# Agent attention with a SoLU layer on one core: u copied by transfer and transposed in rounded fp32, three of five tile pairs transposed on TensorE, and the buffers and queues around that

## The chip, the cores and the metric

The kernel runs on one core of a Trainium2 chip. The metric is the device time of one execution in microseconds, given as the median of the runs. PE is the matrix engine (TensorE), DVE the vector engine, ACT the scalar engine, POOL the general engine (GpSimd), and SP the engine that issues the transfers (DMAs).

## The reference

Four batches of 12,608 tokens with 128 channels; 49 agents per batch; a feed-forward width of 1,024.

```python
a2k = sm(agents, k); agent_v = a2k @ v        # per batch: 49 x 128
x = sm(q, agents) @ agent_v                   # sm: softmax of the scaled product
h = x @ w_in
solu = h * softmax(h)
ln = (solu - mean) / sqrt(var + 1e-06) * g_ln
out = ln @ w_out
```

`w_in` and `w_out` come as 64-bit floats and are converted to 32-bit ones on the chip.

## The kernel before, in words

All work is cut into operations that the class `Plan` (L26) puts in order when the program is built: each `op(engine, function, cost, due, dependencies)` has a price and a due time, and a list scheduler writes the instructions of each engine in the order that comes out. On the chip every engine runs its own list strictly in that order. SP's list of transfers is ordered in the same way, and a transfer whose source isn't ready holds all transfers behind it on SP. Four PSUM banks `px` are handed out by the plan; two further tiles `ph` (two banks each) hold the rows of `h`.

**Phase A** (`phase_a`, once per batch) walks over k and v in 12 chunks of 1,024 tokens and a rest: load k and v (`kop`, `vop`), logits (L465), running maximum (L470), exp (L491), transpose (L498), copy to SBUF (L504), product with v (L514), and the sum with a factor (L523). At the end the product of the agents' values with `w_in` is written as a high and a low part, `mh` and `ml` (L585, L590), each 128 x 1024 in rounded fp32 (fp32r). `mh` and `ml` have two buffers. For the first batch (the head), nothing else runs meanwhile but the conversion of the weights.

**Phase B** (`phase_b`, once per 8 token tiles) makes the softmax p of the queries over the agents: logits (L694), normalised values in `pack` (L722, POOL), two transposes per four tiles (L729), a copy from PSUM (L737, ACT), a split into high and low part on POOL (L743, L748), and four to eight transfers on SP that put them, one below the other, into `pT` (L767).

**Phase C** runs over 396 tiles of 128 tokens:
- `c_h` (L824): four matmuls give 128 x 1024 of h in `ph`; `c_max` (L828, DVE), `c_exp` (L838, ACT, into a tile `e`), `c_u` (L843, DVE): u = h * e / 1024 in a tile `u` (two buffers); `c_sq` (L849, ACT): the sum of squares.
- Tiles go in pairs, and pairs have two kinds; `PAT` gives the order. A **Z** pair transposes u on TensorE (`c_t`, L856, eight 128 x 128 blocks of fp32 per tile), ACT copies the result to SBUF (`c_ev`, L907), POOL splits it into a high and a low part in fp32r (`c_sph` L916, `c_spl` L920), and 24 matmuls of 256 columns per pair (`c_w`, L937) multiply with the split `w_out`. A **Y** pair is transposed in 32 x 32 blocks by DVE (`c_tb`, L863), the blocks are put in their places by 16 transfers per group of four tiles (`c_mv`, L871), and 32 fp32 matmuls per group (`c_wy`, L877) multiply with `w_out`.
- Groups of four tiles (two pairs of a kind, called units) share a chain of small POOL operations that gives the factor 1/std per token (`c_rstd`, L951 to L972). A Z group turns it with DVE (L976), sends it to DRAM and reads it back as a row repeated on all partitions (`send` L980, `sent` L984); `c_fin` (L1020, DVE) multiplies and `c_out` (L1025) stores. A Y group needs it per partition: POOL makes `dy` (L1002), TensorE sums (L1007), ACT or DVE copies it (`yp`, L1011), and `c_fy` (L885 on ACT, L887 on DVE) multiplies.

With the order ZYZY, and Z for the last four pairs, there are 102 Z pairs and 96 Y pairs.

Of the kernel before, what the change touches and what calls it, by code (L numbers as in the profile page):

```python
# [19 lines left out]
class Op:  # L20


    __slots__ = ("eng", "fn", "cost", "due", "left", "outs", "deps", "take", "free", "bank", "start", "end", "by", "ready", "kind", "shy")


class Plan:  # L26
# [11 lines left out]

    def __init__(self, banks):
# [4 lines left out]
        self.kind = 0  # L44

# [14 lines left out]
    def push(self, o):  # L60
        o.ready = {}
        for e in o.eng:
            o.ready[e] = max([0.0] + [d.end + (self.LAT.get(d.by + e, 0.2) if d.by != "S" else 0.0) for d in o.deps])
            self.cand[e].append(o)

    def run(self, idle=None):
        while True:
            best = None
            for e, ops in self.cand.items():
                if not ops:  # L70
                    continue
                free = [b[0] for b in self.banks if b[0] is not None]
                first = min(free) if free else None
                at, opts, low = self.at[e], [], None
                for o in ops:
                    s = max(at, o.ready[e])
                    if o.take:
                        if first is None:
                            continue
                        s = max(s, first)  # L80
                    opts.append((s, o))
                    low = s if low is None else min(low, s)
                if low is None:
                    continue
                near = [z for z in opts if z[0] <= low + self.EPS[e]]
                if e == "P" and self.kind == 2:
                    near = [z for z in opts if z[0] <= low + self.HOLD and z[1].kind == 2] or near
                s, o = min(near, key=lambda z: z[1].due)
                if o.shy > 0.0:
                    s, o = min((z for z in opts if z[0] <= s + o.shy), key=lambda z: z[1].due)  # L90
                if best is None or s < best[0]:
                    best = (s, e, o)
            if best is None:
                break
            s, e, o = best
            for z in o.eng:
                self.cand[z].remove(o)
            if o.take:
# [5 lines left out]
            o.start, o.by = s, e  # L104
            if e == "S":
                hold, size, lag = o.cost
                self.at[e] = s + hold
# [24 lines left out]
PAT = "ZYZY"  # L132
# [18 lines left out]
def kernel(  # L151
# [15 lines left out]
    P = 128  # L167
# [9 lines left out]
    CPR = 5.63  # L177
    UTB = 3
# [9 lines left out]
    BD0 = 5.03  # L188
    BD1 = 15.85
    BD2 = 1.88  # L190
    BD3 = -20.87
    BD4 = -3.24
    BD5 = 3.07
    DH = -9.08
    DMX = 6.59
    DEX = 1.64
    DU_ = -21.8
    DSQ = 15.3
    DT = -0.97
    DEV = 13.79  # L200
    DLD = 12.64
    DSP = 16.84
    DW = 13.2
    DR = 15.79
    DF_ = 37.93
    OUTD = 20.02
    OUTC = -69.6
    VA = 3
    VA1 = 12
    QA = 22.03  # L210
    WA = -7.03
    VLAG = 0.74
    PTB = 4
    SHY = 0.31
    DHR = 5.82
    DHL = -9.02
    DMXR = 19.87
    DMXL = 0.06
    DEXR = -2.43
    DEXL = -3.57  # L220
    DUR = -30.17
    DUL = 17.14
    DSQR = -54.86
    DSQL = 4.96
    DTR = -20.36
    DTL = -14.12
    DEVR = -17.55
    DEVL = 7.51
    DLDR = -20.48
    DLDL = -18.62  # L230
    DSPR = -1.34
    DSPL = -11.65
    DWR = -2.28
    DWL = 3.97
    RBL = 2.38
    ASP = 0.86
    MZ = 5.66
    B7G = True
    B7 = 7.35
    DTB = 4.24  # L240
    DMV = -0.75
    DMS = 0.0
    MVC = 2
    DWY = 11.65
    DWS = 4.05
    YC = 2
    DFY = 5.09
    DTBR = -5.14
    DTBL = -8.26
    ASTART = -4.09  # L250
    AEND = 0.95
# [20 lines left out]
    make_identity(nc, ident)  # L272
    ones = const.tile([P, P], F32, name="ones")
# [13 lines left out]
    def pair_f64(dst, names):  # L287
# [5 lines left out]
        def tmp():  # L293
            for k, tg in (("s", "e"), ("a", "e"), ("e", "u"), ("m", "u")):
                t = epool.tile([P, 2, HW], I32, tag=tg, bufs=2, name=f"c{k}_{names}")
# [39 lines left out]
    def load_out():  # L335
        nc.sync.dma_start(out=g_sb, in_=g_ln)
        for h in range(2):
            wd = words["out", h] = mpool.tile([P, HW, 2], I32, tag="mh" if h == 0 else "ml", name=f"wd_out{h}")
# [6 lines left out]
    def conv_out():  # L345
# [8 lines left out]
        def sums(q):  # L354

            n = NF >> (q + 1)
            if q == 0:
                pm["s"] = epool.tile([P, NF // 2, C], F32, tag="sq", bufs=1, name="ws")
# [32 lines left out]
    for i in range(2):  # L391
        pk = const.tile([P, GT, AP2], F32, name=f"pack{i}")
        nc.gpsimd.memset(pk, 0.0)
# [10 lines left out]
    fold32 = const.tile([P, SQB], F32, name="fold32")  # L404
    nc.vector.tensor_reduce(out=fold32, in_=ident.rearrange("p (a c) -> p c a", c=SQB), op=ALU.add, axis=AX.X)
# [838 lines left out]
```

## Time and profile before

| | |
|---|---|
| median of 3 runs | 1501.4 us (1495.41 to 1503.94) |
| the profiled execution | 1496.0 us, span 1494.2 us, granted clock 0.995 |
| PE busy | 1447.1 us, 97% of the span |
| DVE busy | 1371.5 us, 92% |
| ACT busy | 1291.3 us, 86% |
| POOL busy | 1110.3 us, 74% |
| q1 (the transfers of the kernel) | 63.1% of the 16 DMA engines' time |

The profile shows one execution. A busy time is the union of the engine's instructions, so overlapping parts of neighbours count once; a matmul's own duration holds the way through the array, so that neighbours overlap. The pace of matmuls is read from the chain that ended last, where a piece is the time from one group of instructions to the next.

### The profile page before, as it was taken

What the parts mean: (1) busy time and instruction counts of PE and PEld (TensorE: products, weight loads), DVE (VectorE), ACT (ScalarE), POOL (GpSimd) and SP (SyncE); (2) the same over time, 40 slices, a digit from 0 to 9 for tenths busy, and PEclk for the clock granted to TensorE, in tenths of its full rate; (3) what the DMA queues carried; (4) which work ended last, traced back from release to release, by engine and by line L of the source; (5) the groups of instructions that cost most, each with busy time, mean ns of one, the idle gap of its engine ahead of it and who ended that gap; (6) DMA issues with size and microseconds to landing.
All of it is one profiled execution on the core that took longest, in us unless ns stands there. A gap on an engine that the chain in (4) does not pass through costs nothing.

```text
span 1494.2 us, 34108 instructions
## 1 busy us (share of the span) xinstructions
PE 1447.1 (97%) x11954; PEld 1285.0 (86%) x11954; DVE 1371.5 (92%) x1987; ACT 1291.3 (86%) x2536; POOL 1110.3 (74%) x1569
## 2 busy tenths in 40 slices
PE   8889999999999999999999999899999999999999
PEld 5668889898988989989887888789889898989998
DVE  7799999999999999999998898699999999999996
ACT  4688989889988988899887898688899999999995
POOL 2667787788778777787786677677788888888875
PEclk9999999999999999999999999999999999999999
DMA  9565676676577668756657655567546656566461
GB/s 371 163 179 156 177 186 160 174 184 153 144 194 202 165 179 215 181 137 158 155 140 200 184 156 157 147 175 206 138 118 157 152 126 166 137 154 162 114 155 57
DMA packets 142698, 247.72 MB, mean 166 GB/s; under 512 B 26048, under 2 KB 80320, under 8 KB 142528
## 3 DMA queue, kind: packets, MB, share of 16 engines
q1 hardware_dynamic: 142528, 245.54, 63.1%
q8 instruction: 96, 1.57, 0.5%
q14 instruction: 74, 0.61, 0.1%
HBM read 92.77 MB, written 26.05 MB: 80 GB/s over the span
## 4 chain that ended last, share of the span: by engine, by line
PE 56%; ACT 13%; DVE 10%; DMA 10%; issue 5%; SPq 4%; POOL 2%; DVEq 0%; ACTq 0%; POOLq 0%
PE ph L824 15%; PE px L877 14%; PE px L937 11%; PE px L856 6%; ACT e L838 5%; DVE u L843 4%; DMA rB<-dr 4%; ACT sq L849 4%; DVE nm L828 3%; PE px L465 3%; SPq L871 3%; PE px L514 3%; DMA dr<-yr 2%; ACT uT L907 2%; PE px L694 2%
## 5 line engine op out<-in xcount | busy, mean ns | idle before, releaser
L849 ACT ACTIVATE sq<-u,su 128x1024 bf16<-128x1024 f32 x396 | 460.7, 1163 | 53.4 <-DVE u L843 49.2
L843 DVE SCALAR_TENSOR_TENSOR u<-ph,e 128x1024 f32<-128x1024 f32 x396 | 474.6, 1217 | 29.4 <-ACT e L838 13.6
L838 ACT ACTIVATE e<-ph,nm 128x1024 f32<-128x1024 f32 x396 | 442.8, 1124 | 60.6 <-DVE nm L828 58.9
L828 DVE TENSOR_REDUCE nm<-ph 128x1 f32<-128x1024 f32 x396 | 467.8, 1206 | 28.2 <-PE ph L824 26.8
L920 POOL TENSOR_TENSOR uL<-uT,uH 128x1024 fp32r<-128x1024 f32 (+1 forms) x198 | 470.7, 2377 | 14.5
L877 PE MATMUL px<-w,uY 128*128 128x128 f32 x3072 | 383.0, 276 | 1.7 <-ACT uT L907 1.0
L877 PEld LDWEIGHTS px<-w,uY 128*128 128x128 f32 x3072 | 365.9, 192 | 8.7 <-ACT uT L907 2.3
L824 PE MATMUL ph<-mh,pT 128*128 128x512 f32 x792 | 336.5, 425 | 8.6 <-DVE u L843 5.4
L824 PE MATMUL ph<-ml,pT 128*128 128x512 f32 x792 | 312.8, 395 | 0.0
L916 POOL TENSOR_SCALAR uH<-uT 128x1024 fp32r<-128x1024 f32 (+1 forms) x198 | 207.6, 1048 | 99.2 <-ACT uT L907 99.0
L937 PE MATMUL px<-uH,wH 128*128 128x256 f32 x816 | 238.7, 292 | 0.6 <-POOL x L957 0.3
L863 DVE STREAM_TRANSPOSE tb<-u 128x1024 f32<-128x1024 f32 x192 | 237.2, 1238 | 1.3
L937 PE MATMUL px<-uL,wH 128*128 128x256 f32 x816 | 235.7, 289 | 0.0
L907 ACT COPY uT<-px 128x512 f32<-128x512 f32 x394 | 220.8, 595 | 16.7 <-PE px L856 12.9
L937 PE MATMUL px<-uH,wL 128*128 128x256 f32 x816 | 235.0, 288 | 0.0
L856 PE MATMUL px<-ident,u 128*128 128x128 f32 x1632 | 223.0, 274 | 6.8 <-DVE ob L1020 4.0
L856 PEld LDWEIGHTS px<-ident,u 128*128 128x128 f32 x1632 | 191.2, 141 | 33.4 <-DVE ob L1020 5.1
L824 PEld LDWEIGHTS ph<-mh,pT 128*128 128x128 f32 x792 | 149.8, 189 | 43.7 <-DVE u L843 13.5
L824 PEld LDWEIGHTS ph<-ml,pT 128*128 128x128 f32 x792 | 150.1, 189 | 19.5 <-DVE ml L590 0.3
L937 PEld LDWEIGHTS px<-uH,wL 128*128 128x128 f32 x816 | 153.8, 189 | 5.0 <-issue 2.3
L937 PEld LDWEIGHTS px<-uH,wH 128*128 128x128 f32 x816 | 153.9, 189 | 4.8 <-issue 1.3
L937 PEld LDWEIGHTS px<-uL,wH 128*128 128x128 f32 x816 | 154.1, 189 | 4.2 <-issue 1.1
(132 smaller groups left out, 1595.9 us busy)
## 6 DMA issues: line engine op xcount, KB each, us to landing
uY<-tb SPq DMA_DIRECT2D x768, 128.0 KB, 2.9
pT<-pn SPq DMA_DIRECT2D x392, 64.0 KB, 2.2
qt<-in_qT_dram SPq DMA_DIRECT2D x48, 512.0 KB, 4.4
kt<-in_kT_dram SPq DMA_DIRECT2D x36, 512.0 KB, 4.4
vt<-in_v_dram SPq DMA_DIRECT2D x36, 512.0 KB, 4.8
rB<-dr SPq DMA_DIRECT2D x50, 256.0 KB, 3.7
out_dram<-ob SPq DMA_DIRECT2D x50, 256.0 KB, 2.6
out_dram<-oy SPq DMA_DIRECT2D x48, 256.0 KB, 2.8
```

Source lines behind the costliest of these rows:

```text
L824: nc.tensor.matmul(ph[:, sl], lhs, bmats[b]["mh" if m == 0 else "ml"][:, sl], start=(m == 0), stop=(m == 1))
L828: nc.vector.tensor_reduce(out=nms[x], in_=phs[x], op=ALU.max, axis=AX.X, negate=True)
L838: nc.scalar.activation(out=es[x], in_=phs[x], func=AF.Exp, bias=nms.pop(x), accum_out=st[G]["S"][:, j : j + 1])
L843: nc.vector.scalar_tensor_tensor(out=u, in0=phs[x], scalar=INV, in1=es[x], op0=ALU.mult, op1=ALU.mult, accum_out=su)
L849: nc.scalar.activation(out=sq, in_=u, func=AF.Square, bias=su, scale=-float(DF), accum_out=st[G]["Q"][:, j : j + 1])
L856: nc.tensor.transpose(pt[:, kf * P : (kf + 1) * P], us[x][0][:, k0 * P : (k0 + 1) * P], ident)
L863: nc.vector.transpose(to, us[x][0].rearrange("p (k r c) -> p k r c", r=GT, c=SQB))
L877: nc.tensor.matmul(st[G]["po"][:, a * P : (a + 1) * P], yb[G][1][:, a, kf].rearrange("p x c -> p (x c)"), w2[:, kf, :], start=(kf == 0), s ...
L907: nc.scalar.copy(out=rr[x][:, hf * 4 : hf * 4 + 4, :], in_=pt)
L916: nc.gpsimd.tensor_scalar(out=uH, in0=rr[x][:, k0:k1, :], scalar1=1.0, scalar2=0.0, op0=ALU.mult, op1=ALU.add)
L920: nc.gpsimd.tensor_tensor(out=uL, in0=rr[x][:, k0:k1, :], in1=uH.bitcast(F32), op=ALU.subtract)
L937: nc.tensor.matmul(po, wt[:, kf, :], ut[:, kf, :], start=(q == 0), stop=(q == WM - 1))
```

## The change

- The order of pairs becomes ZYZYZ. With Z for the last four pairs there are 120 Z pairs and 78 Y pairs.
- A Z tile's u is copied by a transfer (`c_cp`, 512 KB) from the tile `u` to a tile `uR` of type fp32r (three buffers), and TensorE transposes `uR` against an fp32r identity. `u` has three buffers, `uT` four. The squares of `c_sq` are written over the tile `e` instead of a tile of their own.
- p is split into its high and low part before it is turned: `b4`, `b4h`, `b4l` on POOL; one transpose per tile in fp32r instead of one per two tiles; ACT's copy of 512 columns writes `pT`. The split after the transpose and the transfers of `pT` are gone.
- The factor of a Y group goes through DRAM too (`send`, and `senty`, which reads it as 4-byte elements); `dy`, its matmul and its copy are gone. `rB` has three buffers, and `c_fin` writes its result over `rB`.
- In the head all loads of k are listed ahead of those of v, with other buffers, and the transposed values of all chunks are kept.
- `mh` and `ml` have one buffer: their writing waits for the last `c_h` of the batch before.
- The plan gets operations of the kind "SA", a transfer that SP or ACT may issue; ACT is offered it 30 us after it is ready, and only behind an operation of over 1 us. The due times of most operations get other values.

```diff
-PAT = "ZYZY"
+PAT = "ZYZYZ"
...
+            if e == "A" and o.eng == "SA":
+                o.ready[e] += self.SLACK
...
-    UTB = 3
+    UTB = 4
+    RB_ = 3
+    UBF = 3
...
-    MVC = 2
+    MVC = 1
...
-    mpool = ctx.enter_context(tc.tile_pool(name="mpool", bufs=2))
+    mpool = ctx.enter_context(tc.tile_pool(name="mpool", bufs=1))
...
+    rpool = ctx.enter_context(tc.tile_pool(name="rpool", bufs=RB_))
...
+    identR = const.tile([P, P], F32R, name="identR")
+    nc.vector.tensor_copy(out=identR, in_=ident)
...
-                old = M1.get(c - 1) if not head else M1.get(c - 5 - c % 4)
+                old = M1.get(c - 1) if not head else None
...
-            old = M2.get(c - 1) if not head else M2.get(c - 5 - c % 4)
+            old = M2.get(c - 1) if not head else M1[3] if 4 <= c < 8 else M1[7] if 8 <= c < NCK else None
...
+        for c in range(NC if head else 0):
+            kop(c)
...
-            o9 = op("A", st(f4h, hf), 0.571, at(z + 0.8 + 0.4 * hf), [o8, l0, last_h.get(b - 2)] + mdone[b])
+            o9 = op("A", st(f4h, hf), 0.571, at(z + 0.8 + 0.4 * hf), [o8, l0, last_h.get(b - 1)] + mdone[b])
...
+        def b4h(q):
+            m, d, _ = cut(q)
+            nc.gpsimd.tensor_scalar(out=packs[q][:, :m, 0, :A], in0=d, scalar1=1.0, scalar2=0.0, op0=ALU.mult, op1=ALU.add)
+
+        def b4l(q):
+            m, d, _ = cut(q)
+            nc.gpsimd.tensor_tensor(out=packs[q][:, :m, 1, :A], in0=d, in1=packs[q][:, :m, 0, :A].bitcast(F32), op=ALU.subtract)
+
         def b5(q, px):
...
-            for j in range(0, m, 2):
-                nc.tensor.transpose(px[:, j * AP2 : (j + 2) * AP2], packs[q][:, j : j + 2, :].rearrange("p j a -> p (j a)"),
-                                    ident)
+            for j in range(m):
+                nc.tensor.transpose(px[:, j * P : (j + 1) * P].bitcast(F32R), packs[q][:, j].rearrange("p i a -> p (i a)"), identR)
 
         def b6(q):
...
+            pt = pTs[b, t0 // GT + q] = bpool.tile([P, GT * P], F32R, tag="pT", bufs=PTB, name=f"pT{b}_{t0}_{q}")
+            nc.scalar.copy(out=pt[:, : m * P], in_=r.pop(("pt", q))[:, : m * P])
...
-        sq = epool.tile([P, DF], BF16, tag="sq", bufs=1, name=f"sq{x}")
+        sq = es.pop(x).bitcast(BF16)[:, :DF]
...
+    def c_cp(x, e):
+        rr[x, "u"] = rpool.tile([P, DF], F32R, tag="uR", name=f"uR{x}")
+        port[e].dma_start(out=rr[x, "u"].bitcast(F32), in_=us[x][0])
...
-            nc.tensor.transpose(pt[:, kf * P : (kf + 1) * P], us[x][0][:, k0 * P : (k0 + 1) * P], ident)
+            nc.tensor.transpose(pt[:, kf * P : (kf + 1) * P].bitcast(F32R), rr[x, "u"][:, k0 * P : (k0 + 1) * P], identR)
...
+        def senty(e):
             yp = st[G]["yp"] = tiny.tile([P, GT], F32, tag="yp", name=f"yp{G}")
...
+            port[e].dma_start(out=yp, in_=r["dr"].rearrange("j p -> (j p)").rearrange("(a p) -> p a", p=P))
...
-        U[x] = op("D", F(c_u, x), 1.21, at(x, DU_, DUR, DUL), [EX[x], T.get((x - 2, 0)), T.get((x - 2, 1)), TBT.get(x - 2), SQ.get(x - 2)])
+        U[x] = op("D", F(c_u, x), 1.21, at(x, DU_, DUR, DUL), [EX[x], CP.get(x - UBF), TBT.get(x - UBF), SQ.get(x - UBF)])
...
+            CP[x] = op("SA", F(c_cp, x), (0.5, 0.524, 0), at(x, DCP, DTR, DTL), (cout if zx < RB_ else []) + [U[x], T.get((xo, 0)), T.get((xo, 1))])
             for hf in range(2):
-                T[x, hf] = op("P", F(c_t, x, hf), 0.435, at(x, DT, DTR, DTL) + 0.02 * hf, [U[x]] + buf, take=True)
+                T[x, hf] = op("P", F(c_t, x, hf), 0.28, at(x, DT, DTR, DTL) + 0.02 * hf, [CP[x]] + buf, take=True)
```

## Rows read from the trace of the kernel before

**Rows 1.** The page's first part: busy time of each engine, its share of the span, and its instructions.
```profile
span 1494.2 us, 34108 instructions
PE 1447.1 (97%) x11954; PEld 1285.0 (86%) x11954; DVE 1371.5 (92%) x1987; ACT 1291.3 (86%) x2536; POOL 1110.3 (74%) x1569
```

**Rows 2.** Busy time by stretch: from and to, length, then the busy us of PE, PEld, DVE, ACT and POOL with their instructions, the granted clock, the DMA share and GB/s. The first row is the kernel between head and tail, the second its busiest long stretch.
```profile
100.00:1440.00 1340.00, 1310.92 (x10813) 1181.20 (x10812) 1252.59 (x1779) 1191.21 (x2332) 1033.14 (x1455) 1.00 0.64 163
...
1000.00:1300.00 300.00, 296.85 (x2454) 270.04 (x2453) 287.90 (x404) 273.23 (x530) 243.35 (x337) 1.00 0.61 151
```

**Rows 3.** The chain that ended last, from 640 to 673 us: start, length, engine, tile, line and number of instructions. Length by number is the pace. (An fp32 matmul of L877 is two records.)
```profile
640.37 0.12 PE px L1007 x2
...
664.44 1.79 PE px L877 x16
666.23 1.85 PE ph L824 x8
...
669.00 2.39 PE px L937 x20
671.39 0.87 PE px L856 x8
672.26 0.22 PE px L729 x2
```

**Rows 4.** Waits and what followed one. First who waited for whom: us in total, number of times, longest us; then two stretches in the form of Rows 2.
```profile
DVE ob L1020 <- DMA rB<-dr: 30.2, 18, 8.3
...
PE px L498 <- DVE ob L1020: 8.6, 2, 7.6
...
920.00:940.00 20.00, 12.41 (x94) 11.41 (x93) 11.41 (x18) 11.74 (x24) 8.69 (x15) 0.93 0.39 119
940.00:960.00 20.00, 20.00 (x161) 17.31 (x160) 17.18 (x26) 16.29 (x33) 13.95 (x17) 0.89 0.72 173
```

**Rows 5.** Groups of instructions on DVE by line and shape: count, busy us and mean ns of one, then idle time before them.
```profile
L863 DVE STREAM_TRANSPOSE tb<-u 128x1024 f32<-128x1024 f32 x192 | 237.2, 1238 | 1.3
...
L1020 DVE TENSOR_TENSOR ob<-px,rB 128x512 f32<-128x512 f32 x50 | 34.2, 684 | 30.2 <-DMA rB<-dr 30.2
...
L976 DVE STREAM_TRANSPOSE yr<-ycol 128x32 f32<-128x32 f32 x50 | 9.9, 197 | 0.0
...
L887 DVE TENSOR_TENSOR oy<-px,yp 128x512 f32<-128x512 f32 x14 | 9.5, 682 | 2.0 <-PE px L877 2.0
```

**Rows 6.** The same view, ACT. (The four instructions of L885 serve one group.)
```profile
L907 ACT COPY uT<-px 128x512 f32<-128x512 f32 x394 | 220.8, 595 | 16.7 <-PE px L856 12.9 <-POOL z L963 1.7 <-POOL pack L722 0.6
...
L885 ACT ACTIVATE oy<-px,yp 128x128 f32<-128x128 f32 x136 | 38.7, 370 | 0.4
L737 ACT COPY pf<-px 128x256 f32<-128x256 f32 x100 | 38.1, 387 | 7.3 <-PE px L729 7.2
...
L1011 ACT COPY yp<-px 128x4 f32<-128x4 f32 x34 | 5.6, 165 | 0.7 <-PE px L1007 0.6
```

**Rows 7.** The same view, POOL.
```profile
L920 POOL TENSOR_TENSOR uL<-uT,uH 128x1024 fp32r<-128x1024 f32 x196 | 468.1, 2389 | 14.3
...
L916 POOL TENSOR_SCALAR uH<-uT 128x1024 fp32r<-128x1024 f32 x196 | 206.3, 1053 | 99.2 <-ACT uT L907 99.0
...
L748 POOL TENSOR_TENSOR pn<-pf,pn 128x256 fp32r<-128x256 f32 x100 | 73.7, 737 | 7.7
...
L743 POOL TENSOR_SCALAR pn<-pf 128x256 fp32r<-128x256 f32 x100 | 41.0, 410 | 31.0 <-ACT pf L737 29.0 <-DMA out_dram<-ob 1.5
```

**Rows 8.** Transfers. First the queue's packets, MB and share of the 16 engines; then SP's own timeline (start, length, line, transfer, count): one burst of 16; then two stretches in the form of Rows 2, the first with a load to and stores from 128 partitions, the second in that burst; last, issues by line with KB of one and the median us to landing.
```profile
q1 hardware_dynamic: 142528, 245.54, 63.1%
...
724.01 10.74 SPq L871 DMA_DIRECT2D uY<-tb  x16
...
722.00:724.00 2.00, 2.00 (x13) 1.63 (x12) 2.00 (x5) 1.61 (x4) 1.92 (x2) 1.00 0.99 362
730.00:732.00 2.00, 2.00 (x13) 1.25 (x12) 2.00 (x3) 2.00 (x4) 1.92 (x2) 1.00 0.97 217
...
uY<-tb SPq DMA_DIRECT2D x768, 128.0 KB, 2.9
pT<-pn SPq DMA_DIRECT2D x392, 64.0 KB, 2.2
...
kt<-in_kT_dram SPq DMA_DIRECT2D x36, 512.0 KB, 4.4
```

**Rows 9.** The head and the end of a phase A: a piece of the chain that ended last (six matmuls of the first tiles' `c_h`), SP's last loads of v in the head, and the groups that write `mh` and `ml`.
```profile
58.07 1.57 PE ph L824 x6
...
35.14 3.14 SPq L459 DMA_DIRECT2D vh<-in_v_dram  x3
...
L590 DVE SCALAR_TENSOR_TENSOR ml<-px,rs,mh 128x512 fp32r<-128x512 f32 x8 | 5.9, 739 | 1.4 <-ACT mh L585 1.4
L585 ACT ACTIVATE mh<-px,rs 128x512 fp32r<-128x512 f32 x8 | 5.5, 694 | 0.7 <-DVE wL L377 0.7
```

More of the change, by code (lines that the diff above doesn't have):

```diff
@@ L20 @@
 class Op:
-    __slots__ = ("eng", "fn", "cost", "due", "left", "outs", "deps", "take", "free", "bank", "start", "end", "by", "ready", "kind", "shy")
+    __slots__ = ("eng", "fn", "cost", "due", "left", "outs", "deps", "take", "free", "bank", "start", "end", "by", "on", "ready", "kind", "shy")
 class Plan:
@@ L63, in push, with pick @@
             o.ready[e] = max([0.0] + [d.end + (self.LAT.get(d.by + e, 0.2) if d.by != "S" else 0.0) for d in o.deps])
+            if e == "A" and o.eng == "SA":
+                o.ready[e] += self.SLACK
             self.cand[e].append(o)
+            self.old.add(e)
+    def pick(self, e):
+        ops = self.cand[e]
+        if not ops:
+            return None
+        first = None
+        if e == "P":
+            free = [b[0] for b in self.banks if b[0] is not None]
+            first = min(free) if free else None
+        at, opts, low = self.at[e], [], 1e9
+        for o in ops:
+            s = o.ready[e]
+            if o.eng == "SA":
+                if e == "A" and not self.long:
+                    continue
+                if s < at:
+                    s = at
+                if e == "S":
+                    s += self.LEAN
+            elif s < at:
+                s = at
+            if o.take:
+                if first is None:
+                    continue
+                if s < first:
+                    s = first
+            opts.append((s, o))
+            if s < low:
+                low = s
+        if not opts:
+            return None
+        top = low + self.EPS[e]
+        near = [z for z in opts if z[0] <= top]
+        if e == "P" and self.kind == 2:
+            near = [z for z in opts if z[0] <= low + self.HOLD and z[1].kind == 2] or near
+        s, o = min(near, key=self.rank)
+        if o.shy > 0.0:
+            s, o = min((z for z in opts if z[0] <= s + o.shy), key=self.rank)
+        return s, e, o
@@ L66, in run, with rank @@
+    @staticmethod
+    def rank(z):
+        return z[1].due
     def run(self, idle=None):
+        now, self.old = {}, set(self.cand)
         while True:
+            for e in self.old:
+                now[e] = self.pick(e)
+            self.old = set()
             best = None
[L69 to L92, printed above, removed]
@@ L93, in run @@
+            for e in self.cand:
+                if now[e] is not None and (best is None or now[e][0] < best[0]):
+                    best = now[e]
             if best is None:
@@ L95, in run @@
             s, e, o = best
+            if e == "S" and o.eng == "SA":
+                s -= self.LEAN
+            self.old.add(e)
             for z in o.eng:
                 self.cand[z].remove(o)
+                self.old.add(z)
+            if o.take or o.free is not None:
+                self.old.add("P")
             if o.take:
@@ L103, in run @@
                 idle(s - self.at[e])
-            o.start, o.by = s, e
-            if e == "S":
+            o.start, o.by, o.on = s, e, e
+            if e == "A":
+                self.long = o.eng != "SA" and (o.cost[o.eng.index(e)] if len(o.eng) > 1 else o.cost) > 1.0
+            if e == "S" or o.eng == "SA":
                 hold, size, lag = o.cost
-                self.at[e] = s + hold
+                o.by = "S"
+                self.at[e] = s + (hold if e == "S" else 0.05)
                 if size:
```

337 lines of the change are left out of this document (152 added, 185 removed).

## The prediction

> **What bounds it now.** I read the busy times first: PE 97%, DVE 92%, ACT 86%, POOL 74% [rows 1]. A share over the whole span says little here, so the stretches come next. Between head and tail (100 to 1440 us) PE is busy 97.8%, DVE 93.5%, ACT 88.9%, POOL 77%; in the best long stretch PE is at 99.0%, DVE at 96.0% and ACT at 91.1% [rows 2]. The chain that ended last confirms PE: where nothing goes wrong it is matmul after matmul at a steady pace, whatever the other engines do [rows 3]. So PE's work sets the time of an undisturbed stretch, with DVE 3 to 4 points behind. Disturbances start on SP: DVE waited 30.2 us for the factor `rB`, and behind one such wait PE stood 7.6 us for a bank; in the stretch that holds the longest wait PE was busy 12.4 of 20 us, and the granted clock was 0.93 there and 0.89 in the next [rows 4]. A stall of PE is paid a second time by matmuls at the lower level.
>
> **The change on PE.** Paces [rows 3]: transpose of u 0.87/8 = 0.109 us, of p 0.22/2 = 0.11, a record of L877 1.79/16 = 0.112, a 256-column fp32r matmul 2.39/20 = 0.1195, a 512-column one 1.85/8 = 0.231, the small `dy` matmul 0.12/2 = 0.06.
> No row shows an fp32r transpose of 128 columns. From 512 to 256 columns the pace falls by 0.112, so 128 columns fewer again take off 0.056: 0.0635. Below, 0.06 is the pace of the `dy` records, which load 128 x 128 weights and stream 4 columns. Above, 0.109: no gain at all. I take 0.07, close to the fp32r rows; it is also what the diff's plan asks (0.28 for four), and the plan's old price, 0.435 for four, agrees with 4 x 0.109.
> - Transposes of u: 102 x 16 = 1632 at 0.109 become 120 x 16 = 1920 at 0.07: 177.9 to 134.4, -43.5.
> - Transposes of p: 200 at 0.11 become 396 at 0.07: +5.7.
> - Y matmuls: 9 groups fewer (48 to 39), 64 records each: 576 x 0.112 = -64.5.
> - Z matmuls: 18 pairs more, 24 each: 432 x 0.1195 = +51.6.
> - `dy`: 96 records at 0.06: -5.8.
>
> Sum **-56.5 us**; with 0.06, -79.5; with 0.109, +34.
>
> The pace of 0.06 says that loading 128 columns of fp32 weights doesn't hold TensorE for more than that. The Trainium skill (TensorE: Matmul & The Clock Gate, section LDWEIGHTS) speaks against the change: it puts a load at the number of columns over 1.2 ns, an estimate of 107 ns for 128 columns. By that rule the transposes would stay where they are and PE's sum would be +34; the `dy` rows [rows 3] disagree with it.
>
> **On DVE.** 36 Y tiles fewer: 36 x 1.238 = -44.6. `c_fin` 50 to 59: +6.2. Turning the factor 50 to 98: 48 x 0.197 = +9.5. `c_fy`, if DVE keeps its 14 of 48: 11.4 of 39, -1.8. Sum **-30.7**; if DVE takes all 39, -13.6 [rows 5].
>
> **On ACT.** Copies of half a tile 408 to 480: 72 x 0.595 = +42.8. The copy of p grows from 256 to 512 columns: 100 x (0.595 - 0.387) = +20.8. The `yp` copies go: -5.6. `c_fy` at ACT's share, 34 of 48: 6.4 fewer at 38.7/34 = 1.14: -7.3. Sum **+50.7** [rows 6]. The squares written over `e` cost nothing new: same instruction, but `e` comes free only after `c_sq`.
>
> **On POOL.** 36 Z tiles more at 1.053 + 2.389: +124. The split of p is on 196 instead of 256 elements a row and in two steps as before, so it costs no more than its 115 us [rows 7]. POOL ends near 1230 us, 85% of the time forecast: covered by its own slack, since 99 us of its idle time is waiting for ACT's copies.
>
> **On the transfers.** A copy of u, 128 rows of 4 KB, has no row. Below: 512 KB at the 362 GB/s of a stretch with transfers on 128 partitions, 1.45 us; above: at the 217 GB/s of the Y bursts, 2.42 us [rows 8]. 240 copies take 348 to 580 us. Gone are 144 Y transfers at 10.74/16 = 0.67 us (-97) and 25.7 MB of `pT` (-71 to -118). From 63.1% of 1494 = 943 us that makes 1076 to 1355 us, 75 to 94% of the time forecast. I take the low end, since the copy uses all 128 partitions as the faster stretch does, and a Y transfer only 32. SP issues 400 `pT` and 144 Y transfers fewer and 240 + 48 + 39 more, some 217 x 0.67 = 145 us less.
>
> The copy is a new wait: the transposes now wait for `c_cp`, and `c_u` three tiles on waits for it as well. Behind the transpose in PE's list stand `c_h` and all other matmuls, so a late copy stops PE. A tile takes 1494/396 = 3.8 us; three tiles less one `c_u` give 10 us, against issue and landing of about 0.67 + 4.4 (a 512 KB load [rows 8]): 5 us to spare. This covers a copy that SP issues in time.
>
> **Head and ends of phases A.** The first `c_h` starts at 58.07; the last v is issued up to 38.28 [rows 9]. With k first, the work on k (maximum, exp, transposes) is done when v comes, and only the product is left behind the last load; the bytes are the same. Estimate: -5, between 0 and -12. With one buffer, `mh` and `ml` are written after the last `c_h`: 0.93 (four matmuls) + 0.694 + 0.739 = 2.4 us for the first half, 3.8 for the second [rows 3, 9], against the 3.8 us of a tile that `c_h` waits for `c_u` anyway. Three times 1 us: +3, up to +10 uncovered.
>
> **The sum.** PE alone would give -56.5 between head and tail. DVE needs 1252.6 - 30.7 = 1222 us there: at its best share so far (96.0%) 1273 us, at its mean share (93.5%) 1307, against 1340: -67 to -33. The wait for `rB` has fewer transfers ahead of it and more buffers, which speaks for the better share; three engines at once near their limits speak for the other. Middle: -50. 1496.0 - 50 - 5 + 3 = **1444 us** for the profiled execution. The median before lies 5.4 us above that execution, so I put the median at **1446**.
>
> **Rivals.**
> - *ACT becomes the bound.* Its work between head and tail becomes 1242 us; at 91.1%, its best so far, that is 1363 us (+23), at DVE's 96% 1294 (-46). Middle -11: 1496 - 11 - 2 = 1483. For it: ACT already waits for DVE in small pieces that a static order can't fill. Against: it was never asked for more, and its busy time shrinks when copies run back to back. Chance 0.12.
> - *Slower: copies late behind Y bursts.* A burst of 16 holds SP for 10.74 us [rows 8]; a copy listed behind a whole one eats the 5 us to spare and stops DVE or PE for about 6 us. 39 bursts: at one in three, 13 x 6 = 78 us, 1496 + 78 - 52 = 1522. It decides from 52/6 = 9 bursts on. For it: the 30.2 us that `rB` waited the same way. Against: SP has 145 us less to issue, and with MVC = 1 other transfers may stand between. Chance 0.12.
> - *fp32r transposes bring nothing.* The change doesn't do what it says: 1496 + 34 - 2 = 1528. This is the case of the rule on weight loads. Against: the pace of `dy`. Chance 0.07.
> - *A little of everything:* stalls eat the gain and the time stays within 0.5%. Chance 0.05.
>
> **The numbers.** The forecast has 0.64, with a range of its own from 1415 (PE at 0.06 leaves DVE's 96% as the limit: -67, head -12) to 1472 (-33, head 0, +10). ACT's case lies above it, most of it under 1490. 1412 to 1490 holds both, about 0.78 with what the other cases spill into it; the two slow cases stay outside. 0.5% is 7.5 us, about what a measurement of this kernel can tell from no change. Faster by more: 0.64, 0.10 of ACT's case and 0.03 of the bursts (fewer than nine late), 0.77. Same: 0.05 and 0.02 of ACT's, 0.07. Slower: 0.09 and 0.07, 0.16.
>
> **What would show it.** Transposes of u in runs of eight at 0.56 instead of 0.87 us; 1920 of them; 156 block transposes on DVE; ACT busy near 1340 us; DVE at 94% or more between head and tail; the wait for `rB` gone or under 10 us; DMA share near 0.75. It is wrong if the transposes keep 0.109, if `c_u` or the transposes wait for the copy for more than 20 us in total, or if ACT is over 95% and DVE waits for `e`.

## The result, and the profile after

The changed kernel takes 1507.8 us (median of 20 runs, 1503.2 to 1515.4) against 1499.3 us for the kernel before (20 runs, 1494.3 to 1505.6): a ratio of 1.006, 95% interval 1.0045 to 1.0076. It is slower by 0.6%. The forecast was 1446 us, with a range of 1412 to 1490.

Its profiled execution took 1506.9 us (before 1496.0). First the page's busy times, the queue, and the issues of the two large groups of transfers inside the core (KB of one, median us to landing); they answer to [rows 1] and [rows 8].

```profile
span 1505.1 us, 34195 instructions
PE 1433.5 (95%) x12173; PEld 1265.7 (84%) x12173; DVE 1351.7 (90%) x2006; ACT 1317.4 (88%) x2512; POOL 1198.9 (80%) x1593
...
q1 hardware_dynamic: 137280, 329.07, 71.5%
...
uR<-u SPq DMA_DIRECT2D x240, 512.0 KB, 3.9
uY<-tb SPq DMA_DIRECT2D x624, 128.0 KB, 3.2
```

PE is busy 14 us less and DVE 20, and both shares fell: no engine took PE's place as the bound. The stretch between head and tail, in the form of [rows 2], says the same:

```profile
100.00:1440.00 1340.00, 1290.51 (x10969) 1156.33 (x10968) 1225.07 (x1781) 1206.83 (x2287) 1107.86 (x1446) 0.99 0.73 220
```

PE was busy 1290.5 of 1340 us (1310.9 before). So there is less work, but also more standing. To part the two I take from the trace, for every matmul record, the time until the next one starts; where this is over 0.2 us above the median of its kind, the median counts as work and the rest as standing. PE's work goes from 1400.1 to 1382.1 us (-18.0), its standing from 89.6 to 116.2 us (+26.6). The sum, +8.6, is most of the 10.9 us between the two profiled executions. (The split is good to a few us: with a kind for each line and its tiles the same rule gives -18.9 and +27.5.)

The pace of the transposes is read from the chain that ended last (start, length, engine, tile, line, number), as in [rows 3]:

```profile
606.17 0.63 PE px L890 x8
...
609.36 1.96 PE px L973 x16
611.32 0.30 PE px L890 x4
611.62 0.51 PE px L913 x4
...
672.50 0.29 PE px L799 x4
```

Eight transposes of u take 0.63 us: 0.079 each, against 0.109 before and the 0.07 (0.56 for eight) of the forecast. Record by record, the first two of a run start 0.060 and 0.064 us apart, and from the third on it is a steady 0.084.

The waits (who for whom: us in total, times, longest us), first DVE's and PE's, which answer to [rows 4], then those of SP's queue:

```profile
DVE nm L858 <- PE ph L854: 51.6, 76, 3.5
DVE u L873 <- ACT e L868: 31.4, 86, 1.6
DVE rB L1044 <- DMA rB<-dr: 10.8, 7, 3.4
...
DVE u L873 <- DMA uR<-u: 3.6, 5, 1.1
...
PE px L890 <- DMA uR<-u: 7.6, 6, 2.0
PE px L973 <- DVE rB L1044: 5.7, 3, 3.1
...
SPq L884 <- DVE u L873: 161.6, 84, 7.9
SPq L907 <- DVE tb L897: 59.0, 14, 8.5
...
SPq L1017 <- DMA dr<-yr: 44.7, 30, 4.2
```

The new first place on SP's queue is the copy of u (L884), which waits for `c_u` 84 times, 161.6 us in total. How such a wait can reach PE is seen near 1331 us. SP's timeline, then the chain there, then that stretch in the form of [rows 2]:

```profile
1326.96 0.69 SPq L1035 DMA_DIRECT2D yp<-dr  x1
1331.33 0.50 SPq L884 DMA_DIRECT2D uR<-u  x1
1331.88 0.58 SPq L1017 DMA_DIRECT2D rB<-dr  x1
```

```profile
1331.60 0.23 SPq L884
1331.83 0.05 issue
1331.88 3.88 DMA rB<-dr
1335.76 0.02 issue
1335.78 0.70 DVE rB L1044
1336.48 0.14 issue
1336.62 3.39 PE px L973 x15
```

```profile
1330.00:1350.00 20.00, 16.66 (x131) 14.74 (x130) 14.61 (x20) 15.37 (x31) 13.89 (x10) 0.84 0.30 104
```

SP stands from 1327.65 to 1331.33 for u; the read of the factor stands behind it, lands 3.88 us after its issue, DVE multiplies, and only then are there banks for PE. The factor itself had landed in DRAM at 1328.94, so its read went out 2.9 us late. Then, after PE has stood 3.1 us, fifteen matmuls take 3.39 us, 0.226 each where sixteen took 1.96 us (0.1225) at 609 us: the granted clock of the stretch is 0.84, part of it at the lower level. Two more reads stand in the same way directly behind a copy that waits for u: they are issued at 1292.25 and 1406.38, 2.1 and 3.8 us after the factor had landed. These three make 9.5 of DVE's 10.8 us.

Where in the kernel it is lost: `c_u` of the first tile of each batch (0, 99, 198, 297) starts at 62.2, 416.3, 770.9 and 1150.9 us before and at 61.5, 419.7, 773.6 and 1129.1 after; that of the last tile at 1479.2 and 1485.5; the spans end at 1494.2 and 1505.1. By batch, with PE's work and standing after, less those before (a kind for each line and its tiles):

| batch | us before | us after | PE's work | PE's standing |
|---|---|---|---|---|
| 1 | 354.1 | 358.2 | -9.2 | +13.2 |
| 2 | 354.6 | 353.9 | -7.5 | +7.1 |
| 3 | 380.0 | 355.5 | -11.4 | -13.2 |
| 4 | 328.2 | 356.4 | +2.4 | +25.7 |

The first two batches gain nothing: the work that PE saves comes back as standing. The third gains 24.5 us, over half of it standing that the kernel before has there, with its disturbed stretch of [rows 4]. The last loses 28.2 us, nearly all of it standing, and the tail 4.5.

### The profile page after: what moved, and what is told of

The parts are those of the page before. It is cut to its first block, busy times and chain, and to the rows that moved or that the text cites. A ratio compares the mean times of both kernels' runs of the same rounds, so it can differ in the third digit from the quotient of the medians.

```text
span 1505.1 us, 34195 instructions
## 1 busy us (share of the span) xinstructions
PE 1433.5 (95%) x12173; PEld 1265.7 (84%) x12173; DVE 1351.7 (90%) x2006; ACT 1317.4 (88%) x2512; POOL 1198.9 (80%) x1593
## 3 DMA queue, kind: packets, MB, share of 16 engines
q1 hardware_dynamic: 137280, 329.07, 71.5%
## 4 chain that ended last, share of the span: by engine, by line
PE 67%; DVE 10%; DMA 8%; ACT 7%; issue 4%; SPq 2%; POOL 1%; DVEq 0%; ACTq 0%; POOLq 0%
PE ph L854 19%; PE px L973 17%; PE px L913 16%; PE px L890 7%; DMA uR<-u 4%; DVE u L873 3%; ACT e L868 3%; DVE nm L858 3%; PE px L754 2%; PE px L510 2%; PE px L564 2%; SPq L907 2%; ACT e L879 2%; DMA rB<-dr 1%; ACT uT L943 1%
## 5 line engine op out<-in xcount | busy, mean ns | idle before, releaser
L956 POOL TENSOR_TENSOR uL<-uT,uH 128x1024 fp32r<-128x1024 f32 (+1 forms) x234 | 558.8, 2388 | 18.3
L858 DVE TENSOR_REDUCE nm<-ph 128x1 f32<-128x1024 f32 x396 | 474.1, 1211 | 53.0 <-PE ph L854 51.6
L868 ACT ACTIVATE e<-ph,nm 128x1024 f32<-128x1024 f32 x396 | 444.8, 1127 | 68.2 <-DVE nm L858 61.5
L879 ACT ACTIVATE e<-u,su 128x1024 bf16<-128x1024 f32 x396 | 460.4, 1167 | 23.4 <-DVE u L873 23.0
L913 PE MATMUL px<-w,uY 128*128 128x128 f32 x2496 | 340.4, 280 | 3.6 <-DMA uY<-tb 1.9
L913 PEld LDWEIGHTS px<-w,uY 128*128 128x128 f32 x2496 | 308.2, 191 | 19.5 <-issue 10.1
L943 ACT COPY uT<-px 128x512 f32<-128x512 f32 x467 | 262.5, 598 | 31.6 <-PE px L890 25.1
L973 PE MATMUL px<-uH,wH 128*128 128x256 f32 x960 | 279.3, 291 | 6.7 <-DVE rB L1044 5.7
L973 PE MATMUL px<-uH,wL 128*128 128x256 f32 x960 | 273.8, 285 | 0.0
L890 PE MATMUL px<-identR,uR 128*128 128x128 f32 x1920 | 215.1, 246 | 21.3 <-DMA uR<-u 7.6
L890 PEld LDWEIGHTS px<-identR,uR 128*128 128x128 f32 x1920 | 194.9, 141 | 46.2 <-ACT uT L943 6.5
L897 DVE STREAM_TRANSPOSE tb<-u 128x1024 f32<-128x1024 f32 x156 | 192.1, 1237 | 1.2
```

What stands on the lines that cost most here:

```text
L858: nc.vector.tensor_reduce(out=nms[x], in_=phs[x], op=ALU.max, axis=AX.X, negate=True)
L868: nc.scalar.activation(out=es[x], in_=phs[x], func=AF.Exp, bias=nms.pop(x), accum_out=st[G]["S"][:, j : j + 1])
L879: nc.scalar.activation(out=sq, in_=u, func=AF.Square, bias=su, scale=-float(DF), accum_out=st[G]["Q"][:, j : j + 1])
L890: nc.tensor.transpose(pt[:, kf * P : (kf + 1) * P].bitcast(F32R), rr[x, "u"][:, k0 * P : (k0 + 1) * P], identR)
L897: nc.vector.transpose(to, us[x][0].rearrange("p (k r c) -> p k r c", r=GT, c=SQB))
L913: nc.tensor.matmul(st[G]["po"][:, a * P : (a + 1) * P], yb[G][1][:, a, kf].rearrange("p x c -> p (x c)"), w2[:, kf, :], start=(kf == 0), s ...
```

## The experiments

My theory after this reading: the transposes save less than was counted, and the copies, waiting for u at the head of SP's list, make other transfers late. Rivals: the landing of the copies, their bytes on the DMA engines, the mix of pairs as such, or the order of the instructions.

### What fp32r transposes are worth

**t_fp32**: `uR` stays an fp32 tile and its transposes are fp32, the order unchanged.

```diff
...
-            nc.tensor.transpose(pt[...].bitcast(F32R), rr[x, "u"][...], identR)
+            nc.tensor.transpose(pt[...], rr[x, "u"][...], ident)
```

> The changed kernel with one thing put back: u's copy and its identity are plain fp32, so the 1920 transposes of u run in fp32. The order of all instructions, the copies and their waits stay. Theory P (the pace of TensorE sets the time): a transposing record goes from the 0.0825 us that it takes in the changed kernel to the 0.109 us of before, 1920 x 0.0265 = +51 us of work, and most of it shows: 1508 + 40 to 55 = 1548 to 1563. Theory Q (the order on SP's list and the waits behind it set the time, TensorE has slack): less than half of it shows, 1510 to 1530.

1530.2 us, ratio 1.0217 (1.0174 to 1.0259). The 1920 transposes take 200.2 us, 0.104 each, instead of 158.4 (0.0825); the time is 22 us longer. So the fp32r form does work, and of 42 us on PE it brings about half to the end; PE stands some 17 us less here than in the changed kernel. PE isn't the bound all the time, and the time lies between the two ranges, at the edge of the second.

### What the copies cost

**no_copy**: no copies; the transposes read a constant tile of zeros, so u is left out of the Z pairs' product.

```diff
...
-        rr[x, "u"] = rpool.tile([P, DF], F32R, tag="uR", name=f"uR{x}")
-        port[e].dma_start(out=rr[x, "u"].bitcast(F32), in_=us[x][0])
+        rr[x, "u"] = uconst
```

> The changed kernel without the 240 transfers of u: TensorE transposes a tile that is filled once with zeros, so the output is not the reference's. The order of instructions on the engines stays, SP issues 240 transfers fewer and nothing waits for them. Theory Q (copies that wait for u hold the transfers behind them on SP, and transposes wait for copies): the 27 us by which TensorE's standing time grew go, 1508 - 20 to -30 = 1478 to 1488. Theory P: standing time has other reasons (factor, DVE), 1500 to 1508.

1483.8 us, ratio 0.991 (0.9881 to 0.9939): 24 us below the changed kernel. Standing on PE falls from 116.2 to 97.9 us. DVE still waits 8.0 us for the factor (10.8 in the changed kernel):

```profile
DVE rB L1045 <- DMA rB<-dr: 8.0, 2, 6.1
```

**no_factor_read**: the transfers of `sent`, which read the factor of a Z group back, are left out, and nearly all Z groups are multiplied by ones.

```diff
-            port[e].dma_start(out=rB.rearrange("d a j p -> d (a j p)"),
-                              in_=r["dr"].rearrange("j p -> (j p)").unsqueeze(0).to_broadcast([P, P * GT]))
...
```

> The changed kernel without the 59 transfers that read the factor of a Z group back as a row on all partitions: the product takes ones instead, so the output lacks the factor. All else stays, the sending too. If DVE's wait for that transfer (10.8 us, all in the last batch) and the 9 us of TensorE's standing behind that product are what the changed kernel lost there: 1508 - 8 to -14 = 1494 to 1500. If other waits take its place: 1503 to 1508.

1495.2 us, ratio 0.9983 (0.9963 to 1.0003): 12.7 us below the changed kernel. With these transfers go their bytes too, and SP's own waiting at them (44.7 us at L1017 in the changed kernel), so the 12.7 us are not a price of the copies alone.

**copy_unused**: the copies are issued as before and wait for u, but the transposes turn the identity, so nothing waits for a copy except buffers. **copy_const_source**: the other way round; the copies read a constant tile (`wL`, filled with zeros), so they wait for no u, move the same bytes, and the transposes wait for them. In both, u is left out of the Z pairs.

```diff
-            nc.tensor.transpose(pt[...].bitcast(F32R), rr[x, "u"][...], identR)
+            nc.tensor.transpose(pt[...].bitcast(F32R), identR, identR)
```

```diff
+    nc.gpsimd.memset(wL.bitcast(F32), 0.0)
...
-        port[e].dma_start(out=rr[x, "u"].bitcast(F32), in_=us[x][0])
+        port[e].dma_start(out=rr[x, "u"].bitcast(F32), in_=wL.rearrange("p k c -> p (k c)").bitcast(F32))
```

> The changed kernel with all 240 copies of u issued, waiting for u and landing as before, but nobody reads them: TensorE transposes the identity instead, so the output is not the reference's. Without any copies the kernel took 1484 us. Theory H (a copy that stands at the head of SP's list and waits for u holds the factor's read-back, the Y transfers and the stores behind it): the cost stays, 1498 to 1508. Theory L (transposes stand until the copy has landed): the cost is gone, 1482 to 1490.

> The changed kernel with the 240 copies at their places on SP's list, as large as before, and with the transposes waiting for them, but their source is a weight tile that doesn't change, so no copy waits for u, and u is free without them; the output is not the reference's. Theory H (holding SP while waiting for u): the cost goes, 1480 to 1490. Theory L (landing) or B (the bytes themselves, 126 MB on the DMA engines): it stays, 1498 to 1508.

1502.4 us, ratio 1.0033 (1.0017 to 1.0049), and 1479.9 us, ratio 0.9881 (0.9847 to 0.9915). Copies that wait for u cost 22 us although nobody needs them (and a constant in the place of u gains nothing by itself, since copy_unused has one too); copies that are needed but don't wait cost nothing against no_copy, with the same bytes. What the landing costs the transposes is at most the 5 us between the changed kernel and copy_unused. DVE's wait for the factor, and what SP's queue waits for at the copies (L884, in the second L885), in copy_unused and then in copy_const_source:

```profile
DVE rB L1044 <- DMA rB<-dr: 12.0, 6, 3.4
...
SPq L884 <- DVE u L873: 125.3, 70, 8.4
```

```profile
DVE rB L1045 <- DMA rB<-dr: 0.9, 1, 0.9
...
SPq L885 <- PE px L891: 150.3, 80, 5.9
```

The factor comes late 6 times or once; but in no_copy, which is about as fast as copy_const_source, DVE's wait for it was 8.0 us, so it isn't the only way. And SP stands at the copies in the second kernel too, now for a free `uR`, and longer: the sum of SP's waiting doesn't price anything. I read it so, and no run shows it: where a copy waits for a buffer that an earlier tile frees, SP is further ahead in its list than where it waits for the newest u, and what follows on the list is issued earlier.

**unused_four_u** and **unused_u_before**: copy_unused with four buffers of u (and two of `uR`), the order unchanged; in the second the copies read the u of the tile before.

```diff
...
-    rpool = ctx.enter_context(tc.tile_pool(name="rpool", bufs=RB_))
+    rpool = ctx.enter_context(tc.tile_pool(name="rpool", bufs=2))
...
-        us[x] = (epool.tile([P, DF], F32, tag="u", bufs=UBF, name=f"u{x}"), ...
+        us[x] = (epool.tile([P, DF], F32, tag="u", bufs=UBF + 1, name=f"u{x}"), ...
```

```diff
...
-        port[e].dma_start(out=rr[x, "u"].bitcast(F32), in_=us[x][0])
+        port[e].dma_start(out=rr[x, "u"].bitcast(F32), in_=us[x - 1 if x - 1 in us else x][0])
```

> copy_unused (the copies of u wait for u and move it, but the transposes turn a constant, so u is left out of the Z pairs; 1502 us) with a fourth buffer of u on the chip and two instead of three of uR; the order of the instructions is the same. With it c_u hardly ever waits for a copy to free its buffer (7.9 us in copy_unused). If the cost lies in SP's list, it stays: 1495 to 1505. If it lies in the copies that hold u's buffers, it goes: 1480 to 1488.

> As unused_four_u, but 238 of the 240 copies read the u of the tile before, which has long been written when SP comes to the copy; the same bytes, the same place in SP's list, still waiting for a tile of u. If the cost is SP standing still for the newest u, SP's waiting for u falls from some 125 us to under 50 and the time by 15 to 25 us against unused_four_u, to 1475 to 1487. If traffic or buffers make the cost, it stays within 5 us of unused_four_u.

1499.0 us, ratio 1.0006 (0.9986 to 1.0025): of the 22 us, the buffers of u hold some 3, within the intervals. The second, 1509.8 us, ratio 1.0085 (1.0057 to 1.0113), tells nothing on the theory: SP's queue still waited 123.7 us for u at the copies (128.9 in the first), against the under 50 that I expected, and DVE now waited 34.3 us for ACT's squares. The edit didn't make the state that was to be tried.

### The mix, the prices and the order

**mix_alone**: the kernel before with the new mix. **old_mix**: the changed kernel with the old one.

```diff
-PAT = "ZYZY"
+PAT = "ZYZYZ"
```

> The kernel before with one change: the order of pairs is ZYZYZ, so 120 Z and 78 Y pairs, with u transposed in fp32 from its own tile, p as before. Theory P: TensorE's work changes by 288 x 0.109 (transposes) + 432 x 0.1195 (products of Z) - 576 x 0.112 (products of Y) - 5.8 = +12.7 us, so 1499 + 8 to +20 = 1507 to 1519. Were DVE the bound (36 block transposes fewer, -31 us): 1475 to 1490.

> The changed kernel with the old order of pairs, ZYZY: 102 Z and 96 Y pairs; copies, transposes in fp32r, split of p, factor through DRAM all stay. TensorE's work against the kernel before: 1632 x (0.0825 - 0.106) = -38 on u, +16 on p, -8 without the sum for Y groups, so -30; DVE's work is 10 us more than before. Theory P (TensorE's work sets the time): 1499 - 20 to -30 = 1470 to 1480. Theory D (DVE, now 99% of what it had, takes over): 1495 to 1515.

1601.0 us, ratio 1.0714 (1.0633 to 1.0794), and 1560.5 us, ratio 1.0416 (1.0381 to 1.0451): both far outside what I expected. Their standing on PE is 167.7 and 169.8 us. In mix_alone, `c_u` waits 60.7 us for the transposes that free its two buffers. Neither prices the mix. I take them as a sign that due times chosen for one list are worth little on another; the runs don't part that from the mix itself.

**price_as_measured**: the plan is told what the transposes take, with the due times unchanged. **sp_margin**: the same, and SP is taken to hear of DVE's end 1.0 us late.

```diff
...
-                T[x, hf] = op("P", F(c_t, x, hf), 0.28, at(x, DT, DTR, DTL) + 0.02 * hf, [CP[x]] + buf, take=True)
+                T[x, hf] = op("P", F(c_t, x, hf), 0.345, at(x, DT, DTR, DTL) + 0.02 * hf, [CP[x]] + buf, take=True)
```

```diff
-            "AA": 0.0, "AG": 0.17, "GP": 0.25 + MARGIN, "GD": 0.1, "GG": 0.1, "GA": 0.2}
+            "AA": 0.0, "AG": 0.17, "GP": 0.25 + MARGIN, "GD": 0.1, "GG": 0.1, "GA": 0.2, "DS": 1.0}
...
```

> The changed kernel with two prices of the plan set to what the changed kernel's trace shows: 0.345 instead of 0.28 for four transposes of u, 0.35 instead of 0.28 for four of p. Work and transfers stay, only the order of the lists follows from the new prices; the due times are the old ones. If the wrong price is why engines meet stalls: 1485 to 1500. If an order is as good or bad as its due times happen to make it: anywhere within 1.5% of 1508, 1490 to 1530.

> The run price_as_measured (1521 us) with one entry more in the plan's table of latencies: what DVE releases for SP is taken as 1.0 us later than it ends (0.2 before), so that a copy of u takes its place in SP's list later, behind transfers that can go at once. Theory H (a copy that stands at the head of SP's list and waits for u holds up what is behind it): SP's waiting for u falls from 164 us to under 120 and the time by 10 to 30 us, to 1490 to 1511. Rival (what counts is the whole order, which any change throws over by some 20 us either way): SP's waiting for u falls as well, but the time may lie anywhere from 1500 to 1540.

1521.2 us, ratio 1.0147 (1.0116 to 1.0178), and 1519.3 us, ratio 1.0161 (1.0095 to 1.0227). The margin did not shorten SP's waiting for u (164.3 and 175.2 us), so that prediction of the theory failed. It may be that the copies only moved within SP's list and that SP came to them as early as before; the run doesn't show it.

**order_anew**, **order_other**: the measured prices, and all due times chosen anew with them, from two starts (61 values, a few shown; order_other's plan was somewhat worse). **order_anew_margin**: the same with the 1.0 us, chosen anew again.

```diff
-    DU_ = -25.15
+    DU_ = -49.2
-    DT = -2.14
+    DT = -9.0
-    DCP = -0.78
+    DCP = -3.25
...
-    MVC = 1
+    MVC = 2
```

> The changed kernel with the measured prices of the transposes in its plan (0.335 and 0.35 for four instead of 0.28) and all due times chosen anew for them, SP's latency as it was. PE's work stays near 1382 us, against 1400 before. If the loss lies in an order that was made with a price that TensorE doesn't keep, the stalls fall from 116 to about the 90 us of the kernel before and the time to 1475 to 1490, faster than both. If the chip's departure from the plan on SP decides, SP still waits over 130 us for u and the time stays at 1490 to 1515.

> As order_anew, but with the latency of 1.0 us from DVE to SP of sp_margin, and due times chosen anew with it. Theory H: SP waits under 110 us for u, stalls at 75 to 95 us, 1465 to 1485 us and at least 5 us below order_anew. Rival (the price of the transposes alone spoilt the order): no lower than order_anew, 1475 to 1500.

> A second choice of due times for the changed kernel, made in the same way as order_anew from another start, by its plan somewhat worse. If choosing the times with the measured price of the transposes is what helped, 1480 to 1500, below the changed kernel's 1508. If order_anew was one lucky order, anywhere from 1500 to 1525.

1487.8 us, ratio 0.9926 (0.9901 to 0.995); 1485.8 us, 0.9922 (0.9899 to 0.9945); and 1515.8 us, 1.0113 (1.009 to 1.0137). The first two are faster than both kernels and equal within their intervals; the third is slower than either. No run tries the kernel before with due times chosen anew, so how much of the gain over it belongs to the change stays open. The measured price alone didn't help (price_as_measured), nor did it with every choice of due times (order_other): what helped is the order that one choice led to. The 1.0 us brought nothing here either: in order_anew_margin SP waits 156.1 us for u, where the theory asked for under 110, and the time isn't the 5 us below order_anew that it asked for. In order_anew SP waits for u longer than in any other run, while DVE's wait for the factor is halved:

```profile
SPq L884 <- DVE u L873: 209.4, 85, 12.0
...
DVE rB L1044 <- DMA rB<-dr: 4.9, 3, 2.1
```

**order_anew_const**: order_anew with the constant source of copy_const_source (same edit; u is left out of the Z pairs).

> order_anew with the edit of copy_const_source: the 240 copies read a constant tile instead of u, so they wait for no u, move the same bytes and are waited for by the transposes as before; u itself is left out of the Z pairs. If copies that wait for u at the head of SP's list cost some 25 us in any order, as they did in the order of the changed kernel (1502 against 1480), the time falls to 1458 to 1468. If the new due times have already put the copies where their waiting holds nothing that is needed, it stays at 1480 to 1492.

1460.5 us, ratio 0.9749 (0.973 to 0.9767): 27 us below order_anew. The copies' wait for u costs as much in this order as in the other, though DVE's wait for the factor has only 4 us to lose (4.9 to 0.9). Its stretch, in the form of [rows 2], shows PE busier than in the kernel before (1310.9 us), though PE has less work in all (1370.2 against 1400.1):

```profile
100.00:1440.00 1340.00, 1315.37 (x11327) 1185.68 (x11324) 1263.23 (x1846) 1235.00 (x2343) 1142.27 (x1507) 1.00 0.75 227
```

**copies_by_act**: ACT issues the copies, the due times chosen anew for that.

```diff
...
-            CP[x] = op("SA", F(c_cp, x), (0.5, 0.524, 0), ...
+            CP[x] = op("A", F(c_cp, x, "A"), (0.5, 0.524, 0), ...
...
```

> As order_anew, but ACT issues the 240 copies of u instead of SP, and the due times are chosen anew for that. ACT waits for the same u anyway, for the squares; SP's list loses its waiting for u (209 us in order_anew). If SP's list is the place of the cost and an issue holds ACT for a tenth of a microsecond or less, 1460 to 1480, below order_anew's 1486. If an issue holds ACT as long as it holds SP, 0.5 to 0.67 us, ACT gets 120 to 160 us more to do on top of 1308 and becomes the bound: 1510 to 1560.

1532.8 us, ratio 1.0213 (1.0183 to 1.0244). The time lies in the second range, but not for its reason. ACT is busy 1323.6 us (86%), and its timeline (start, length, line, operation) shows an issue lying beside a running copy:

```profile
603.16 0.58 ACT L943 COPY uT<-px 128x512 f32<-128x512 f32 x1
603.25 0.48 ACTq L884 DMA_DIRECT2D uR<-u  x1
603.78 1.07 ACT L943 COPY uT<-px 128x512 f32<-128x512 f32 x2
```

All 240 issues take 113.8 us, and 82 of these lie beside a running instruction. PE stands 143.1 us in the profiled execution, which was the slowest of the four (1545.3 us). As this order is another one, the run doesn't tell SP's list and the order apart.

## Why the prediction was wrong, point by point

**The pace of an fp32r transpose, the first term of the sum.** I put it at 0.07, next to the 0.06 of `dy` and of the line through the 512- and 256-column matmuls. The row of `dy` was a run of two [rows 3], and 0.06 is not its pace: in the trace of before its two records start 0.03 us apart, the next matmul follows some 0.11 us behind the second, and all 96 take 7.6 us, 0.079 each. Transposes too start 0.060 and 0.064 us apart at the beginning of a run, and then keep 0.084. A pace needs a row with a long run, and the time to what follows. By term, in the trace's own slots (work as split above):

| | forecast | measured |
|---|---|---|
| transposes of u | -43.5 | 172.9 to 158.4: -14.5 |
| transposes of p | +5.7 | 18.2 to 34.7: +16.5 |
| Y matmuls | -64.5 | 333.2 to 271.2: -62.0 |
| Z matmuls | +51.6 | 314.9 to 356.5: +41.6 |
| `dy` | -5.8 | -7.6 |
| `c_h` | 0 | 393.4 to 398.6: +5.2 |
| all PE work | -56.5 | -18.0 |

With the 0.0825 that u's transposes took over all, the forecast's term would have been 158.4 - 177.9 = -19.5 instead of -43.5: the term was mis-sized by 24 us. In the Trainium skill (TensorE: Matmul & The Clock Gate, section Back-to-back issue gap) a stream of load and matmul pairs with 128 columns is put at about 81 ns per matmul; the trace agrees, with 79 in runs of eight and 82.5 over all. The rule of its section LDWEIGHTS that I weighed, an estimate of 107 ns, does not hold here as a floor on the pace, though my reason against it was no pace either.

**"This covers a copy that SP issues in time", the cost of the new wait.** The 5 us to spare were right as far as they go: `c_u` waited 3.6 us for copies in all and the transposes 7.6, both far under 20. But I put the cost of the copies at nothing beyond that. What I didn't count is the other direction, the copy as the one that waits, with transfers queued behind it on SP. Issue time on SP fell, from 913 to 804 us (145 us were worked out), but issue time was not what SP was short of. The price is 22 to 28 us (copy_unused or the changed kernel against copy_const_source; order_anew against order_anew_const; no_copy gives 24). That it is the copies' wait for their source is shown, in two orders; the bytes are excluded, the landing holds at most 5 us and the buffers of u some 3. Without that wait the kernel is 0.9 to 1.2% faster than the kernel before (no_copy, copy_const_source), 13 to 18 us, about what PE's work fell by: the two steps together account for the miss. How the wait reaches PE is shown only in part. In the changed kernel three reads of the factor behind such copies make 9.5 us of DVE's waiting, and without all reads 12.7 us go; but in no_copy and order_anew_const the whole price goes while DVE's wait for the factor falls only from 10.8 to 8.0 and from 4.9 to 0.9. The rest stays open.

**The rivals.** The slower one had the right place, SP's list, with cause and victim exchanged: not copies behind Y bursts but other transfers behind copies, and 22 to 28 us instead of 78. The one on fp32r was wrong for the change; that its 1528 is about what t_fp32 gave (1530) is luck, since PE's work is there some 22 us above the kernel before, not 34, and the rest is standing. ACT did not become the bound: 1317 us, 88%, against the 1342 worked out.

**What was right.** DVE's work fell, by 19.8 us (-30.7 forecast; DVE took 18 of the Y groups' products, not 11); its wait for `rB` from 30.2 to 10.8, as the forecast's middle assumed; POOL went to 1199 us (1230), hidden; the DMA share to 71.5% (75% at the low end). At the three changes of batch PE stood nowhere between the last `c_h` of one batch and the second tile of the next, so the writing of `mh` and `ml` shows no cost there (3 us were put down). Two of the forecast's smaller sums are off: -13.6, if DVE takes all 39 Y products, should be -11.9, and the ends of its inner range, 1415 and 1472, leave out the 5.4 us that the middle was given for the median. Neither decides anything.

**The head** gave about 1 us instead of 5: the first `c_h` starts at 56.60 instead of 57.83 (58.07 is a piece of the chain inside it), the first `c_u` at 61.45 instead of 62.16. There was no load of v to take out of the way: in the kernel before, the chain from 25 us to the first `c_h` holds matmuls and small operations and no load. Now the split of p, moved ahead of its turn, stands in the chain: four transposes of p, listed among the matmuls of the first `c_h`, wait for it. The chain before, then after:

```profile
46.49 1.02 PE px L514 x16
...
55.30 1.72 PE px L578 x4
57.02 0.51 PE px L729 x4
```

```profile
55.94 0.52 POOL logits L785
...
56.53 0.37 POOL pack L789
...
56.98 0.58 POOL pack L793
...
57.60 0.53 PE px L799 x4
```

**The sum again, with what was measured:** 1496.0 - 18.0 (work) + 26.6 (standing) + 2.3 (not parted) = 1506.9 us. The middle of -50 had no term for new standing; it took DVE's share as a limit and let PE's saving through. What stays open is the order itself: six sets of due times or prices for the same instructions (ACT's issue not counted) lie between 1486 and 1521 us, and why PE stands 26 us longer in the last batch of the changed kernel than before, while order_anew, 12 us behind it at tile 297 (1141.6 against 1129.1), is 22 us ahead at the last tile (1463.6 against 1485.5), I can't say from these runs beyond the three late reads of the factor, which all lie in that batch.

## What to carry to other kernels

A transfer that is put in front of an operation is also a transfer that waits for its source, and on an in-order list it makes everything behind it wait too: ask what stands behind it, not only whether it lands in time. A kernel whose order is fixed when it is built has a spread from the order alone, here 35 us, that can be larger than the gain of the change; a new mix or a new price has to be judged with an order made for it, and by more than one. Read a pace from a long run of the instruction itself or of its nearest kind, never from a run of two.

## What the runs showed of the hardware that I had not expected

- A run of fp32r transposes of 128 x 128 starts at 0.060 and 0.064 us and settles at 0.084; fp32 ones keep 0.109 within a run (means over all: 0.106 before, 0.104 in t_fp32). The gain of the form is a quarter at most (0.0825 over all), not the third and more that I forecast.
- The first fp32 matmul directly behind such a run of fp32r transposes holds longer: four records of L913 took 0.51 us at 611.62, where four take 0.45 at 600.72. The median of the first is 0.180 us there (131 times) and 0.110 elsewhere (171); the following ones don't differ.
- 240 copies of 512 KB inside the core take 21 points of the DMA share (50.3% of 1483.9 us in no_copy, 71.5% of 1505.1 here): 330 us of the 16 engines' time, 1.37 us each, under the 1.45 of the forecast's low end. They landed 3.9 us after their issue, less than a load of the same size from DRAM (4.4 us before [rows 8]).
- ACT issues a transfer in 0.48 us while its own instruction runs on.
